# Stores of the first pass and of the output through GpSimd's queue, and G of two batches made in place by 64x32 tiles

## The chip, the core and the metric

One NeuronCore of one Trainium2 chip runs the whole program. The metric is device time in microseconds of one execution; 1384.62 us is the median of three runs of the kernel before (1382.33 to 1386.47). One further execution was recorded with a profile.

## What is computed

Attention of x and a small learned state, in both directions, then two feed-forward layers over all tokens:

```python
def attention(x, state):                      # x [8, 8, 512, 64], state [8, 8, 32, 64]
    s = x @ state.T * 0.125                   # per batch and head
    a = exp(s - s.max(-1)); a /= a.sum(-1) + 1e-9
    xread = a @ state
    s2 = state @ x.T * 0.125
    a2 = exp(s2 - s2.max(-1)); a2 /= a2.sum(-1) + 1e-9
    return concat([xread, a2 @ x], axis=2)    # 544 rows per batch

x = attention(x, state)                       # -> [4352, 512], d_model 512
h = maximum(x @ w_in, 0);   x = (h * h) @ w_out          # d_ff 2048
h = x @ w_in2;              out = (h / (1 + exp(-h))) @ w_out2
```

The four weight matrices arrive as 64-bit floats, and the kernel itself turns their words into 32-bit floats. Products are held to nearly float32 exactness: an operand is split into a rounded part "hi" and a rest "lo", and a product is three matmuls (hi by hi, lo by hi, hi by lo).

## The kernel before, in words

Work on the chip is written as calls that are only recorded. The class `Plan` keeps every operation with its engine, an estimated cost (`cost`, line 107), what it depends on, and the tiles it uses; `order` (line 220) then goes through a model of the engines and picks, one after another, the operation that can start first and is most urgent; `emit` (line 371) issues all instructions in that order. An engine runs its instructions strictly in the emitted order, so where the model is wrong about a time, an engine waits at an instruction although a later one could run. In the model, DMAs are a sixth engine, "dma", all issued by SyncE (SP): 450 ns from one issue to the next, at most 8 in flight (`LANES`), and a slack of 60 us (`DSLACK`) for a transfer that nothing urgent follows. All instructions carry line 186 in the profile, where they are recorded; they are told apart by tile names.

SBUF holds 50 pages of 128x1024 floats and 10 quads of half that size; a page is handed on only when all users of its last tile are done, and a store is a user. PSUM has eight banks: psA and psB (two each) accumulate, psC takes first products, psD takes attention.

The first pass (0 to about 660 us) makes attention and the first feed-forward layer.

- Weights. `sched_conv` (540) loads two raw pages of a weight pair (`c_load`, 490), takes absolute values on ScalarE (`c_abs`, 499), rebuilds the bits on VectorE with seven instructions (`c_bits`, 505), and adds the two parts (`c_sum`, 523) or splits them (`c_split`, 533). `c_store` (530) writes pairs of the second layer's weights to DRAM; `w1_store` (604) writes the first weight matrix for later use.
- G. Since x of the first layer is a @ state, the product with w_in is taken as a @ (state @ w_in). That inner product is called G: 256 rows (8 heads by 32 states) for each batch. `g_unit` (579) makes it for all batches out of one block of w_in: 8 matmuls of 64x64 tiles into the four banks psA and psB, four copies into "go" pages (by ScalarE or VectorE). The rows of batches 0 and 1 lie in the wrong partitions, so four DMAs in each unit move them from the go page to the page Glo of batch and quarter q (name `Glo<-go`); the rest goes to DRAM (`g<-go`) and is loaded when its batch comes (`G_load`, 610). `G_split` (622) then makes Ghi (ScalarE) and Glo (VectorE).
- `scores` (641) makes attention scores of the first three batches with 64x32 tiles, four matmuls in one bank. `sm_first` to `sm1_T` make the softmax and its transpose, the pages AThi and ATlo.
- `gemm1` (767) multiplies G by it (six matmuls into psC), `chain_a` (782) squares and splits, `gemm2` (791) multiplies by w_out in psA and psB. The first three batches (`NB`) go through d_ff in two halves (`PARTS`), so the first half needs G of q 0 and 1 only.
- `evac_a` (820) takes the sums of a Winograd scheme of seven products and stores seven blocks of a batch with 63 DMAs in all (line 838).

The second pass (660 to 1380 us) computes the second layer with those seven products: `gemm3` (968) makes and stores the hidden layer, `gemm4` (1034) makes the output; its `store` (1063) writes it out, the last block (q = 8) in two times four DMAs of 32 rows.

`arith` (451) lets the planner choose between VectorE and GpSimd for elementwise arithmetic; it is called from `split_into`, from the sums and from the softmax.

Of the kernel before, what the change touches and what calls it, by code (L numbers as in the profile page):

```python
# [10 lines left out]
F32 = mybir.dt.float32  # L11
# [16 lines left out]
class Plan:  # L28
# [3 lines left out]

    LATENCY = dict(act=dict(act=153, dve=147, pool=159, pe=265, dma=0),
                   dve=dict(act=128, dve=127, pool=155, pe=256, dma=0),
                   pool=dict(act=150, dve=150, pool=150, pe=309, dma=0),
                   pe=dict(act=197, dve=196, pool=200, pe=3, dma=0),
                   dma=dict(act=0, dve=0, pool=0, pe=100, dma=0))
    LANES = 8  # L40
    WINDOW = 25
    ROUNDS = 3

# [63 lines left out]
    def cost(self, eng, method, writes, reads, args):  # L107
        size = 1
        for ap in writes + reads:
            n = 1  # L110
            for d in ap.shape[1:]:
                n *= d
            size = max(size, n)
        psum = any(self.tiles.get(ap.tensor.name, (0, 0, ""))[2] == "ps" for ap in writes + reads)
        if eng == "dma":
            n = 1
            for d in writes[0].shape:
                n *= d
            return n * 4 / 360
        if eng == "pe":  # L120
            n = 1
            for d in writes[0].shape[1:]:
                n *= d
            if method == "transpose":
                return 109

            share = 128 * 128 // (reads[0].shape[0] * writes[0].shape[0]) if args.get("tile_position") else 1
            return max(n / 2.4 + 13, 109) * (4 if args["rhs"].dtype == F32 else 1) / share
        if eng == "act":
            return (145 if psum else 190) + size / 1.2 + (93 if "accum_out" in args else 0)  # L130
        if eng == "pool":
            return 190 + dict(tensor_tensor=2.2, memset=0.8).get(method, 3.5) * size
        fast = method in ("tensor_scalar", "tensor_copy", "memset") and not psum
        return 157 + size / (1.92 if fast else 0.96)
# [55 lines left out]
    def urgency(self, when=None):  # L190

        ops, n = self.ops, len(self.ops)
        cost = [min(f[1] for f in o["forms"]) for o in ops]
        for i, o in enumerate(ops):
            if o["forms"][0][0] == "dma":
                cost[i] += self.LEAD
        late, t = [], 0.0
        for i, o in enumerate(ops):
            if o["forms"][0][0] == "pe":
                t = when[i] + cost[i] if when else t + cost[i]  # L200
                late.append(t)
            else:
                late.append(t + (self.DSLACK if o["forms"][0][0] == "dma" else self.SLACK))
        before = [list(o["deps"]) for o in ops]
        by_tag = {}
        for t, (tag, users, space) in self.tiles.items():
            if space == "ps" and users and tag:
                by_tag.setdefault(tag, []).append(users)
        for tag, us in by_tag.items():
            us.sort(key=lambda u: u[0])  # L210
            k = self.bufs[tag]
            for a, b in zip(us, us[k:]):
                before[b[0]] += [u for u in a if u < b[0]]
        for i in reversed(range(n)):
            for d in before[i]:
                gap = self.LATENCY[ops[d]["forms"][0][0]][ops[i]["forms"][0][0]]
                late[d] = min(late[d], late[i] - cost[i] - gap)
        return [late[i] - cost[i] for i in range(n)]

    def order(self, when=None):  # L220
# [23 lines left out]
        last_end = {t: (0.0, 0.0) for t in self.tiles}  # L244
        live = set()
        now = dict(pe=600.0, act=1900.0, dve=1070.0, pool=1150.0, dma=600.0)
        ready = {e: [] for e in now}

        def add(i):
            for f in ops[i]["forms"]:  # L250
# [2 lines left out]
        for i in range(n):  # L253
            if not left[i]:
                add(i)
        lanes, hw, wire = [], 0.0, 0.0
        port = dict(dve=0.0, pool=0.0)
        head = 0
        busy, warm = deque(), False
# [3 lines left out]

        def earliest(i, eng):
            o = ops[i]
            e = now[eng]
            for d in o["deps"]:
                e = max(e, end[d] + self.LATENCY[ops[d]["forms"][form[d]][0]][eng])
            need = {}
            for t in fresh(i):  # L270
                need.setdefault(self.tiles[t][0], []).append(t)
            for tag, ts in need.items():
                ahead = 0
                for t in pending[tag]:
                    if t in ts:
                        break
                    ahead += 1
                if ahead + len(ts) > len(free[tag]):
                    return None
                e = max(e, max(x[1] for x in sorted(free[tag])[:len(ts)]) + 150)  # L280
            if eng in port and o["port"][eng]:
                e = max(e, port["pool" if eng == "dve" else "dve"])
            if eng == "dma":
                e = max(e, hw)
                if len(lanes) >= self.LANES:
                    e = max(e, lanes[-self.LANES])
            return e

        done = 0
        while done < n:  # L290
# [4 lines left out]
            for eng, cand in ready.items():  # L295
                mine = []
                low = None
                for _, i in cand[:60]:
# [8 lines left out]
                            continue  # L307
                    mine.append((e, i))
                    low = e if low is None else min(low, e)
                    if e <= now[eng] + self.PATIENCE[eng]:  # L310
                        break
                for e, i in mine:
                    if e <= low + self.PATIENCE[eng]:
                        if best is None or (e, key[i]) < best[:2]:
                            best = (e, key[i], i, eng)
                        break
# [13 lines left out]
            if eng == "pe":  # L330
# [6 lines left out]
                    busy[-1][1] = end[i]  # L337
                else:
                    busy.append([e, end[i]])
            elif eng == "dma":  # L340
                hw = e + 450
                now[eng] = e + 60
                wire = max(wire, e + 1100) + cost
                end[i] = wire + 1500
                lanes.append(end[i])
            else:
                end[i] = now[eng] = e + cost
                if eng in port and o["port"][eng]:
                    port[eng] = end[i]
            for t in o["uses"]:  # L350
                users_left[t] -= 1
                seems = e + self.DMA_SEEMS if eng == "dma" else end[i]
                last_end[t] = max(last_end[t][0], seems), max(last_end[t][1], end[i])
                if not users_left[t] and self.tiles[t][0]:
                    free[self.tiles[t][0]].append(last_end[t])
# [22 lines left out]
def attn_moe_moe_kernel(  # L378
# [12 lines left out]
    P = 128  # L391
# [19 lines left out]

    plan = Plan(dict(page=N_PAGE, quad=N_QUAD, mx1=4, mx2=4, sm1=4, sm2=4))
    V, A, G = plan.engine("dve", nc.vector), plan.engine("act", nc.scalar), plan.engine("pool", nc.gpsimd)
    T, D = plan.engine("pe", nc.tensor), plan.engine("dma", nc.sync)

    def small_tile(shape, tag):
        return plan.tile(small, shape, F32, tag, tag)
# [32 lines left out]

    def arith(op, o, a, b):
        kw = dict(out=o, in0=a, in1=b, op=op)
        plan.either((V, "tensor_tensor", kw), (G, "tensor_tensor", kw))

    def copy(o, a):
        plan.either((A, "copy", dict(out=o, in_=a)), (V, "tensor_copy", dict(out=o, in_=a)))
# [71 lines left out]
            into[key] = c  # L528

    def c_store(key, dst):  # L530
        D.dma_start(dst, cv[key].rearrange("p (k n) -> p k n", k=2))

    def c_split(key, into):
        a, c = cv.pop(key)
# [41 lines left out]

    w1p, gp = {}, {}

    def g_unit(i):
        q, p = divmod(i, 4)  # L580
        g, l = divmod(p, 2)
        pg = w1p[("w1", i // 2)][:, i % 2 * 512:(i % 2 + 1) * 512]
        for bp in range(0, 4, 2):
            ts = [acc_tile(bp), acc_tile(bp + 1)]
            for k in range(2):
                for r in range(2):
                    ps, co = slice(r * 64, (r + 1) * 64), 64 * (r ^ k)
                    T.matmul(out=ts[k][co:co + 64], lhsT=st[ps, bp + k, p].rearrange("p e n -> p (e n)"),
                             rhs=pg[ps], start=True, stop=True, tile_position=(r * 64, co))
            o2 = page(f"go{i}{bp}", F32).rearrange("p (k f) -> p k f", k=2)  # L590
            for k in range(2):
                copy(o2[:, k], ts[k])
            if bp == 0:
                for b in range(2):
                    if (b, q) not in gp:
                        gp[(b, q)] = [None, page(f"Glo{b}{q}")]
                    for r in range(2):
                        D.dma_start(f32(gp[(b, q)][1])[l * 64 + r * NS:l * 64 + (r + 1) * NS, g * 512:(g + 1) * 512],
                                    o2[r * 64 + b * NS:r * 64 + (b + 1) * NS, 0])
                D.dma_start(g_d[q][0][p], o2[:, 1])  # L600
            else:
                D.dma_start(g_d[q][1][p], o2)

    def w1_store(i):
        D.dma_start(w1_d[i], w1p.pop(("w1", i)))

    def w1_load(i):
        w1p[("s", i)] = split_page(f"w1s{i}", 1024, lambda lo: D.dma_start(lo, w1_d[i]))
# [211 lines left out]
    def evac_a(s, j, n):  # L820
# [14 lines left out]

        v.update(sums("b", v, new))
        for i in SEQ:
            at(s + 1, "dma", lambda i=i: D.dma_start(x_d[(i, j)].rearrange("(k p) n -> p k n", p=P), v[SRC_B[i]]))

    def s_tokens_split():  # L840
        hi, lo = page("srhi"), page("srlo")
# [192 lines left out]
    def gemm4(q):  # L1034
# [28 lines left out]
        def store(t, z):  # L1063
            if q < B:
                r0 = q * NT + t * 256
                D.dma_start(out[r0:r0 + 256, :].rearrange("(b p) d -> p b d", p=P), z)
            else:
                for i in range(4):
                    r0 = (4 * t + i) * NT + S
                    D.dma_start(out[r0:r0 + NS, :], z[i * NS:(i + 1) * NS, 0, :])  # L1070

        z = [new(f"z{t}") for t in range(2)]
        ls, hs = slice(0, 256), slice(256, 512)
# [70 lines left out]
    for i in range(NC // 2):  # L1144
# [9 lines left out]
        at(max(n, k + 3) + 1, "late", w1_store, i)  # L1154
        if i == 0:
            at(-12, "dma", load_st)
        at(n, "pe", g_unit, 2 * i)
        at(n, "pe", g_unit, 2 * i + 1)
    for g in range(2):
# [14 lines left out]
    for b in range(NB):  # L1174
        for q in range(4):
            n = slot(b, 4 * q)
            if b >= 2:
                at(n - 6, "dma", G_load, b, q)
            at(n - 3, "vec", G_split, b, q)

    for b in range(NB, B):
        for g in range(2):
# [115 lines left out]
```

## Time and profile before

| what | us |
|---|---|
| median of three runs | 1384.62 |
| the profiled execution | 1381.88 |
| its span, from first to last instruction | 1380.1 |
| TensorE (PE) busy | 1335.8 |
| VectorE (DVE) busy | 1056.3 |
| ScalarE (ACT) busy | 701.0 |
| GpSimd (POOL) busy | 48.9 |

The span is cut out of the profiled execution, which is 1.8 us longer. Times of instructions come from that one execution. An engine is busy from the start of an instruction to its end; "idle before" is the time that an engine stood still ahead of an instruction, with the work whose end let it go on. SPq is SyncE's queue, where all DMAs of this kernel are issued. A float32 matmul of the tiles with 64 rows is recorded as two instructions. Windows are in microseconds from the span's start.

### The profile page before, as it was taken

What the parts mean: (1) busy time and instruction counts of PE and PEld (TensorE: products, weight loads), DVE (VectorE), ACT (ScalarE), POOL (GpSimd) and SP (SyncE); (2) the same over time, 40 slices, a digit from 0 to 9 for tenths busy, and PEclk for the clock granted to TensorE, in tenths of its full rate; (3) what the DMA queues carried; (4) which work ended last, traced back from release to release, by engine and by line L of the source; (5) the groups of instructions that cost most, each with busy time, mean ns of one, the idle gap of its engine ahead of it and who ended that gap; (6) DMA issues with size and microseconds to landing.
All of it is one profiled execution on the core that took longest, in us unless ns stands there. A gap on an engine that the chain in (4) does not pass through costs nothing. (4 is left out here: it accounts for less than half of the span.)

```text
span 1380.1 us, 19261 instructions
## 1 busy us (share of the span) xinstructions
PE 1335.8 (97%) x6892; PEld 1107.9 (80%) x6892; DVE 1056.3 (77%) x1598; ACT 701.0 (51%) x1080; POOL 48.9 (4%) x41
## 2 busy tenths in 40 slices
PE   5889999999999999999999999999998999999998
PEld 1457588888888888888988888999787888888887
DVE  6979488878898888875898866777887676665664
ACT  5755776555555646554662434244455444344442
POOL 0000001110000000000020000000111000000000
PEclk9999999999999999999999999999999999999999
DMA  8761764436264546342759956667899666665663
GB/s 302 262 244 62 223 219 131 123 120 216 80 198 127 168 144 194 112 153 107 225 177 328 363 208 233 248 233 255 280 338 362 195 215 231 220 204 187 201 205 114
DMA packets 206959, 283.08 MB, mean 205 GB/s; under 512 B 13456, under 2 KB 148112, under 8 KB 206864
## 3 DMA queue, kind: packets, MB, share of 16 engines
q1 hardware_dynamic: 206864, 281.86, 61.4%
q8 instruction: 54, 0.88, 0.3%
q14 instruction: 41, 0.34, 0.1%
HBM read 161.35 MB, written 116.26 MB: 201 GB/s over the span
## 5 line engine op out<-in xcount | busy, mean ns | idle before, releaser
L186 ACT ACTIVATE rg<-psC 128x512 f32<-128x512 f32 (+1 forms) x144 | 82.6, 574 | 199.0 <-PE psC L186 195.6
L186 PE MATMUL psC<-AThi,Ghi 128*128 128x512 f32 x256 | 101.6, 400 | 6.0 <-ACT rg L186 3.1
L186 DVE TENSOR_TENSOR gact<-rg,gact 128x512 fp32r<-128x512 f32 (+1 forms) x139 | 90.9, 656 | 19.0 <-ACT rg L186 12.8
L186 PE MATMUL psC<-ATlo,Ghi 128*128 128x512 f32 x256 | 101.1, 398 | 2.2 <-DVE ATlo L186 2.2
L186 PE MATMUL psC<-AThi,Glo 128*128 128x512 f32 x256 | 101.1, 399 | 1.7 <-DVE Glo L186 1.7
L186 ACT ACTIVATE gact<-rg 128x512 fp32r<-128x512 f32 (+1 forms) x144 | 87.7, 609 | 6.9 <-DMA g<-go 3.4
L186 DVE TENSOR_TENSOR rg<-rg 128x512 f32<-128x512 f32 (+1 forms) x66 | 43.7, 662 | 48.4 <-ACT rg L186 48.0
L186 PEld LDWEIGHTS psC<-AThi,Ghi 128*128 128x128 f32 x256 | 48.1, 188 | 21.4 <-ACT AThi L186 4.6
L186 DVE TENSOR_TENSOR W<-psD,U 128x512 f32<-128x512 f32 (+2 forms) x57 | 35.4, 631 | 35.9 <-PE psD L186 35.8
L186 PEld LDWEIGHTS psC<-AThi,Glo 128*128 128x128 f32 x256 | 48.0, 188 | 16.2 <-issue 3.3
L186 PEld LDWEIGHTS psC<-ATlo,Ghi 128*128 128x128 f32 x256 | 48.2, 189 | 14.8 <-DVE ATlo L186 2.9
L186 ACT ACTIVATE r<-r 128x1024 f32<-128x1024 f32 (+2 forms) x20 | 18.6, 932 | 73.3 <-DVE r L186 61.8
L186 DVE TENSOR_SCALAR cv<-cv 128x1024 f32<-128x1024 f32 (+1 forms) x64 | 43.4, 686 | 8.2 <-ACT cv L186 7.9
L186 ACT ACTIVATE rg<-rg 128x512 f32<-128x512 f32 (+1 forms) x78 | 46.3, 594 | 0.0
L186 DVE TENSOR_TENSOR U<-psB,U 128x512 f32<-128x512 f32 (+2 forms) x57 | 35.0, 629 | 14.1 <-PE psB L186 12.6
L186 DVE TENSOR_TENSOR W<-psC,U 128x512 f32<-128x512 f32 (+2 forms) x40 | 24.2, 609 | 27.6 <-PE psC L186 27.2
L186 ACT ACTIVATE cv<-raw 128x512 f32<-128x512 f32 x64 | 40.7, 668 | 8.9 <-DMA raw<-in_w_dram 8.9
L186 PE MATMUL psA<-cc,st 64*64 64x512 f32 x128 | 25.9, 641 | 17.7 <-DVE cc L186 17.3
L186 DVE SCALAR_TENSOR_TENSOR cc<-raw,cv 128x512 int32<-128x512 int32 x64 | 41.9, 684 | 1.4 <-DMA g<-go 1.2
L186 DVE SCALAR_TENSOR_TENSOR cv<-raw,cv 128x512 f32<-128x512 uint32 x64 | 41.5, 682 | 0.2
L186 DVE TENSOR_TENSOR Glo<-Glo,Ghi 128x1024 fp32r<-128x1024 f32 x31 | 37.7, 1216 | 1.2 <-ACT Ghi L186 1.0
L186 ACT COPY U<-psA 128x512 f32<-128x512 f32 (+2 forms) x57 | 28.9, 538 | 14.9 <-PE psA L186 14.3
(1244 smaller groups left out, 4276.2 us busy)
## 6 DMA issues: line engine op xcount, KB each, us to landing
raw<-in_w_dram SPq DMA_DIRECT2D x64, 512.0 KB, 6.4
t<-s SPq DMA_DIRECT2D x36, 512.0 KB, 5.0
Glo<-g SPq DMA_DIRECT2D x96, 128.0 KB, 4.6
t<-r SPq DMA_DIRECT2D x24, 512.0 KB, 4.6
xTr<-in_xT_dram SPq DMA_DIRECT2D x16, 512.0 KB, 8.3
g<-go SPq DMA_DIRECT2D x16, 512.0 KB, 5.7
xnr<-in_xN_dram SPq DMA_DIRECT2D x16, 512.0 KB, 5.6
x<-yt SPq DMA_DIRECT2D x32, 256.0 KB, 4.0
```

Of the source, the lines that this page charges most:

```text
L186: lambda engine=engine, method=method, a=a, k=k: getattr(engine, method)(*a, **k)))
```

## The change

Stores of converted weights, of G, of the seven blocks and of the output are issued by GpSimd (`DS`) in place of SyncE (`D`). The planner gets an engine "sdma" for them: it takes GpSimd's time, 1000 ns for each (`ISSUE`), with 8 lanes of its own. `arith` is VectorE's alone, so GpSimd keeps its memsets and the DMAs. The hidden layer's stores in `gemm3` and those of `w4_sums` stay with SyncE.

For batches 0 and 1 and the quarters q 0 and 1 a new function makes G directly in the layout that `gemm1` reads: four matmuls of 64x32 tiles for each batch and block, a copy to Ghi by ScalarE and a subtraction to Glo by VectorE, both from PSUM. For these units `g_unit` leaves out the two matmuls, the copy and the four DMAs of batches 0 and 1, and `G_split` is not called for them.

```diff
+    ISSUE = 1000
...
-        ready = {e: [] for e in now}
+        clock = dict({e: e for e in now}, sdma="pool")
+        ready = {e: [] for e in clock}
...
-            elif eng == "dma":
-                hw = e + 450
-                now[eng] = e + 60
-                wire = max(wire, e + 1100) + cost
+            elif eng in self.DMA:
+                issue = 450 if eng == "dma" else self.ISSUE
+                hw[eng] = e + issue
+                now[clock[eng]] = e + (60 if eng == "dma" else issue)
+                wire = max(wire, e + 650 + issue) + cost
...
-    T, D = plan.engine("pe", nc.tensor), plan.engine("dma", nc.sync)
+    T = plan.engine("pe", nc.tensor)
+
+    D, DS = plan.engine("dma", nc.sync), plan.engine("sdma", nc.gpsimd)
...
     def arith(op, o, a, b):
         kw = dict(out=o, in0=a, in1=b, op=op)
-        plan.either((V, "tensor_tensor", kw), (G, "tensor_tensor", kw))
+        V.tensor_tensor(**kw)
...
     def c_store(key, dst):
-        D.dma_start(dst, cv[key].rearrange("p (k n) -> p k n", k=2))
+        DS.dma_start(dst, cv[key].rearrange("p (k n) -> p k n", k=2))
...
+    def direct(b, q):
+
+        return b < 2 and 4 * q < PARTS[0][1]
+
+    def g_direct(b, i):
+
+        q, g = divmod(i, 2)
+        if (b, q) not in gp:
+            gp[(b, q)] = [page(f"Ghi{b}{q}"), page(f"Glo{b}{q}")]
+        t = acc_tile(2 * b + g)
+        for l in range(2):
+            for r in range(2):
+                h, ps = 2 * l + r, slice(r * 64, (r + 1) * 64)
+                T.matmul(out=t[h * NS:(h + 1) * NS], lhsT=st[ps, b // 2, 2 * g + l, b % 2],
+                         rhs=w1p[("w1", i)][ps, l * 512:(l + 1) * 512],
+                         start=True, stop=True, tile_position=(r * 64, h * NS))
+        hi, lo = (x[:, g * 512:(g + 1) * 512] for x in gp[(b, q)])
+        A.copy(hi, t)
+        V.tensor_tensor(out=lo, in0=t, in1=hi.bitcast(F32), op=ALU.subtract)
+
     def g_unit(i):
...
         for bp in range(0, 4, 2):
+            ks = (1,) if bp == 0 and direct(0, q) else (0, 1)
             ts = [acc_tile(bp), acc_tile(bp + 1)]
-            for k in range(2):
+            for k in ks:
...
-                for b in range(2):
+                for b in range(2) if 0 in ks else ():
...
-                D.dma_start(g_d[q][0][p], o2[:, 1])
+                DS.dma_start(g_d[q][0][p], o2[:, 1])
             else:
-                D.dma_start(g_d[q][1][p], o2)
+                DS.dma_start(g_d[q][1][p], o2)
 
     def w1_store(i):
-        D.dma_start(w1_d[i], w1p.pop(("w1", i)))
+        DS.dma_start(w1_d[i], w1p.pop(("w1", i)))
...
-            at(s + 1, "dma", lambda i=i: D.dma_start(x_d[(i, j)].rearrange("(k p) n -> p k n", p=P), v[SRC_B[i]]))
+            at(s + 1, "dma", lambda i=i: DS.dma_start(x_d[(i, j)].rearrange("(k p) n -> p k n", p=P), v[SRC_B[i]]))
...
-                    D.dma_start(out[r0:r0 + NS, :], z[i * NS:(i + 1) * NS, 0, :])
+                    DS.dma_start(out[r0:r0 + NS, :], z[i * NS:(i + 1) * NS, 0, :])
...
+        for b in range(2):
+            if direct(b, q):
+                at(n, "pe", g_direct, b, i)
         at(n, "pe", g_unit, 2 * i)
         at(n, "pe", g_unit, 2 * i + 1)
...
-            at(n - 3, "vec", G_split, b, q)
+            if not direct(b, q):
+                at(n - 3, "vec", G_split, b, q)
```

## Rows read from the trace of the kernel before

**Rows 1.** The page: engine, busy us, share of the span, instructions.

```profile
PE 1335.8 (97%) x6892; PEld 1107.9 (80%) x6892; DVE 1056.3 (77%) x1598; ACT 701.0 (51%) x1080; POOL 48.9 (4%) x41
```

**Rows 2.** Windows: length; busy of PE, PEld, DVE, ACT, POOL; granted clock; DMA share; GB/s.

```profile
14.86:48.00 33.14, 28.47 (x160) 6.95 (x160) 26.18 (x44) 22.96 (x44) 0.00 (x0) 1.00 0.71 235
48.00:100.00 52.00, 42.13 (x156) 28.01 (x157) 43.72 (x66) 32.41 (x55) 1.25 (x2) 0.94 0.81 291
100.00:940.00 840.00, 837.42 (x4203) 704.83 (x4203) 675.61 (x1121) 447.54 (x743) 30.71 (x23) 1.00 0.55 182
940.00:1100.00 160.00, 154.45 (x816) 131.16 (x815) 126.06 (x157) 81.41 (x110) 14.46 (x8) 1.00 0.86 292
1340.00:1380.10 40.10, 34.42 (x198) 29.81 (x196) 19.64 (x31) 8.43 (x14) 0.00 (x0) 0.96 0.38 112
```

**Rows 3.** Waits of DVE and ACT before 105 us: total us, times, longest.

```profile
DVE go L186 <- PE psB L186: 5.7, 1, 5.7
DVE cc L186 <- ACT hi('w2', 2)_324 L186: 4.2, 1, 4.2
...
ACT Ghi L186 <- DMA w1d<-cc: 2.2, 1, 2.2
ACT hi('w2', 2)_324 L186 <- DMA g<-go: 2.0, 1, 2.0
```

**Rows 4.** SP's timeline before 105 us: start, length, what is issued.

```profile
17.49 12.71 SPq L186 DMA_DIRECT2D Glo<-go  x8
...
35.49 15.32 SPq L186 DMA_DIRECT2D Glo<-go  x22
50.85 3.94 SPq L186 DMA_DIRECT2D g<-go  x6
...
75.53 2.88 SPq L186 DMA_DIRECT2D g<-go  x3
```

**Rows 5.** PE's timeline, 25 to 81 us: start, length, instruction, count, [idle before].

```profile
25.56 1.09 PE L186 MATMUL psA<-cc,st 64*64 64x512 f32 x8
...
28.36 1.39 PE L186 MATMUL psB<-cc,st 64*64 64x512 f32 x8
...
48.01 0.73 PE L186 MATMUL psC<-AThi,Ghi 128*128 128x512 f32 x2 [1.68 <-ACT AThi L186]
...
73.14 1.04 PE L186 MATMUL psD<-xTr,st 64*32 64x512 f32 x2
74.11 0.50 PE L186 MATMUL psC<-AThi,Glo 128*128 128x512 f32 x1
74.55 1.04 PE L186 MATMUL psD<-xTr,st 64*32 64x512 f32 x2
...
79.89 1.06 PE L186 MATMUL psD<-xTr,st 64*32 64x512 f32 x8
80.89 0.72 PE L186 MATMUL psA<-gact,lo('w2', 2)_325 128*128 128x512 f32 x2
```

**Rows 6.** Groups by form: count, busy us, mean ns, idle before.

```profile
L186 DVE TENSOR_TENSOR Glo<-Glo,Ghi 128x1024 fp32r<-128x1024 f32 x31 | 37.7, 1216 | 1.2 <-ACT Ghi L186 1.0
...
L186 DVE TENSOR_TENSOR a<-psD,a 128x512 fp32r<-128x512 f32 x16 | 11.0, 690 | 4.2 <-ACT a L186 4.1
...
L186 POOL MEMSET sblk<- 128x1024 f32 x2 | 1.8, 951 | 0.0
```

**Rows 7.** Timelines of POOL, DVE and PE around 1065 us.

```profile
1064.65 2.38 POOL L186 TENSOR_TENSOR g110lo<-g110lo,g110hi 128x1024 fp32r<-128x1024 f32 x1 [23.70 <-ACT g110hi L186]
...
1064.81 2.78 DVE L186 TENSOR_TENSOR z<-R 128x512 f32<-128x512 f32 x1
...
1068.24 0.50 PE L186 MATMUL psD<-w,g040hi 128*128 128x512 f32 x1 [1.32 <-DVE W L186]
```

**Rows 8.** SP's timeline at the end of the span, last two rows.

```profile
1374.13 0.82 SPq L186 DMA_DIRECT2D out_dram<-z  x2
1375.01 2.76 SPq L186 DMA_DIRECT2D out_dram<-z  x6
```

More of the change, by code (lines that the diff above doesn't have):

```diff
@@ L28 @@
 class Plan:
[L35 to L39, printed above, removed]
+    LATENCY = dict(act=dict(act=153, dve=147, pool=159, pe=265, dma=0, sdma=153),
+                   dve=dict(act=128, dve=127, pool=155, pe=256, dma=0, sdma=128),
+                   pool=dict(act=150, dve=150, pool=150, pe=309, dma=0, sdma=150),
+                   pe=dict(act=197, dve=196, pool=200, pe=3, dma=0, sdma=197),
+                   dma=dict(act=0, dve=0, pool=0, pe=100, dma=0, sdma=0),
+                   sdma=dict(act=0, dve=0, pool=0, pe=100, dma=0, sdma=0))
+    DMA = ("dma", "sdma")
     LANES = 8
+    ISSUE = 1000
     WINDOW = 25
@@ L114, in cost @@
         psum = any(self.tiles.get(ap.tensor.name, (0, 0, ""))[2] == "ps" for ap in writes + reads)
-        if eng == "dma":
+        if eng in self.DMA:
             n = 1
@@ L194, in urgency @@
         for i, o in enumerate(ops):
-            if o["forms"][0][0] == "dma":
+            if o["forms"][0][0] in self.DMA:
                 cost[i] += self.LEAD
@@ L202, in urgency @@
             else:
-                late.append(t + (self.DSLACK if o["forms"][0][0] == "dma" else self.SLACK))
+                late.append(t + (self.DSLACK if o["forms"][0][0] in self.DMA else self.SLACK))
         before = [list(o["deps"]) for o in ops]
@@ L255, in order @@
                 add(i)
-        lanes, hw, wire = [], 0.0, 0.0
+        lanes, hw, wire = dict(dma=[], sdma=[]), dict(dma=0.0, sdma=0.0), 0.0
         port = dict(dve=0.0, pool=0.0)
@@ L265, in earliest @@
             o = ops[i]
-            e = now[eng]
+            e = now[clock[eng]]
             for d in o["deps"]:
@@ L282, in earliest @@
                 e = max(e, port["pool" if eng == "dve" else "dve"])
[L283 to L286, printed above, removed]
+            if eng in self.DMA:
+                e = max(e, hw[eng])
+                if len(lanes[eng]) >= self.LANES:
+                    e = max(e, lanes[eng][-self.LANES])
             return e
@@ L309, in order @@
                     low = e if low is None else min(low, e)
-                    if e <= now[eng] + self.PATIENCE[eng]:
+                    if e <= now[clock[eng]] + self.PATIENCE[clock[eng]]:
                         break
                 for e, i in mine:
-                    if e <= low + self.PATIENCE[eng]:
+                    if e <= low + self.PATIENCE[clock[eng]]:
                         if best is None or (e, key[i]) < best[:2]:
@@ L339, in order @@
                     busy.append([e, end[i]])
-            elif eng == "dma":
-                hw = e + 450
-                now[eng] = e + 60
-                wire = max(wire, e + 1100) + cost
+            elif eng in self.DMA:
[3 more added lines that the diff above has]
+                wire = max(wire, e + 650 + issue) + cost
                 end[i] = wire + 1500
-                lanes.append(end[i])
+                lanes[eng].append(end[i])
             else:
@@ L351, in order @@
                 users_left[t] -= 1
-                seems = e + self.DMA_SEEMS if eng == "dma" else end[i]
+                seems = e + self.DMA_SEEMS if eng in self.DMA else end[i]
                 last_end[t] = max(last_end[t][0], seems), max(last_end[t][1], end[i])
@@ L590, in g_unit @@
             o2 = page(f"go{i}{bp}", F32).rearrange("p (k f) -> p k f", k=2)
-            for k in range(2):
+            for k in ks:
                 copy(o2[:, k], ts[k])
             if bp == 0:
-                for b in range(2):
+                for b in range(2) if 0 in ks else ():
                     if (b, q) not in gp:
@@ L1065, in store @@
                 r0 = q * NT + t * 256
-                D.dma_start(out[r0:r0 + 256, :].rearrange("(b p) d -> p b d", p=P), z)
+                DS.dma_start(out[r0:r0 + 256, :].rearrange("(b p) d -> p b d", p=P), z)
             else:
```

## The prediction

> **What bounds the kernel now.** I read the engines' totals first. TensorE is busy 1335.8 of 1380.1 us, VectorE 1056.3, GpSimd 48.9 [rows 1]: the kernel can only gain where TensorE stands still, or where it runs slower than it could. So the second view is the windows, and the reader is to subtract TensorE's busy time from the length of each stretch [rows 2]. It starts at 14.86 us. From there to 48 it idles 33.14 - 28.47 = 4.7 us, from 48 to 100 it idles 9.9, from 100 to 940 only 2.6, from 940 to 1100 it idles 5.6, and 5.7 after 1340. From 48 to 100 its granted clock is also a mean of 0.94, that is, part of the stretch ran at the lower level, 1.2 GHz; that costs about 0.06 x 42.1 = 2.5 us. The head of the kernel is where this change can pay.
>
> Third, the waits of the head [rows 3]. VectorE stands still 4.2 us for the split of a weight page by ScalarE, and ScalarE waits 2.0 us there, and 2.2 elsewhere, for stores (of G, of w_in) to release a page. Fourth, SP's own timeline [rows 4] says why these stores are late: the 32 transfers Glo<-go hold the queue from 17.5 to 50.8 us, each behind its copies, and the stores of G come after them, the last issued at 78.4 us. So pages that were ready by 48 us are held for some 30 us more. VectorE idles 52.0 - 43.7 = 8.3 us between 48 and 100 [rows 2]; its conversions feed everything there.
>
> **The change, part by part.** The sum is made against the profiled execution's own 1381.88 us; the median of the runs shown is 2.7 us above it, and I add that at the end.
>
> G in place, TensorE: eight groups (two batches, four blocks) of four 64x32 matmuls are added. Standing together, such a group takes 1.0 us, from 79.89 to 80.89 [rows 5]: +8 us, or 8.5 with its recorded 1.06. Sixteen 64x64 matmuls go. Two units, 32 recorded instructions or 16 matmuls, ran from 25.56 to 29.75 us [rows 5], 0.26 us each: 4.2 us at most, and nothing if the two that are left of a step of four still take the step's time. So TensorE gets 4.3 to 8.5 us of work. It idles 4.7 us in this stretch, but partly because of order. I take the middle, 6.4 - 4.7 = 1.7, and add 0.8 because a bank is now read twice, by the copy and then by a subtraction of 0.69 us [rows 6]: the first product, now at 48.01 us [rows 5], comes **2.5 us later** (bounds 0 and +8.5).
>
> G in place, the others: VectorE loses four subtractions of 1.216 us and gets eight of 0.690 [rows 6], +0.7 us, in the term above. ScalarE's eight copies become eight roundings of the same size, and its four page-wide roundings of Ghi go. SP loses 32 issues, and nothing waits for a landing before the first product; but that product waited for AThi and not for G [rows 5], so the shorter way of G is worth nothing by itself.
>
> Stores on GpSimd, head: there are 143 of them (16 of converted weights, 32 of G, 8 of w_in, 63 of the seven blocks, 24 of the output). No row shows a DMA issued by GpSimd. Its price lies between SP's own spacing at the end, 2.76 / 6 = 0.46 us [rows 8], and GpSimd's longest instruction in the rows, 2.38 [rows 7]; I take 0.95, its memset, which like an issue reads no tensor [rows 6], and the changed planner reckons 1.0. On the whole, 143 x 0.95 = 136 us of an engine that then has nothing else. In the head the stores of q 0 and 1 (16 of G, 4 of w_in) can follow their data, and the loads behind them on SP no longer stand in line. If the pages come free in time, VectorE's 4.2 us go, and with them the pauses ahead of the slow clock, 2.5 us: **-7** (bounds 0, and -10.8 with all 8.3 us of VectorE's idle time and the clock). What is late next is VectorE itself: its busy share from 48 to 100 is 84% already. A store that waits for data on GpSimd holds only later stores, and through them pages; no loads and no arithmetic.
>
> Stores of the seven blocks, of converted weights and of all output blocks but the last: nothing. TensorE's idle time from 100 to 940 is 2.6 us, so what they hold up on SP now is covered by transfers that were issued ahead; if that cover went, 2.6 us is all there is to win.
>
> Arithmetic off GpSimd: 46.4 us of it (48.9 less 2.5 of memsets) go to VectorE at about half the time (1.216 against 2.38 for the same shape [rows 6, 7]), some 24 us over 1000. VectorE is busy 80% from 100 to 940 [rows 2], so this hides beside the matmuls; from 940 to 1100, at 79%, its 14.5 us become 7.4, and I count +0.5 (0 to +2). In return one stall goes: GpSimd's 2.38 us subtraction at 1064.65 stood beside an addition on VectorE that took 2.78 us where its size takes 0.69, and TensorE then waited 1.32 [rows 6, 7]: **-1.3** (bounds 0 and -2.1).
>
> The tail: the last eight stores start at 1374.13 on SP and are issued by 1377.77, and the span ends 2.3 us later [rows 8]. On GpSimd, 8 x 0.95 = 7.6 us from the same start is 1381.7, and with the same 2.3 the end is 1384.1, **+4.0**. Bounds: 0 at SP's price, and +6 at 1.2 us each (eight issues at 2.38 would give +15, but that row reads two full tensors and is far from an issue). Nothing covers this: no other work is left. The Trainium skill (DMA: Bandwidth & Descriptors, Specifications) gives 1 us to the first byte from GpSimd and 0.6 from SP; by its figures, an estimate, the last landing would be 0.4 us later still, +4.4. No row here shows that.
>
> Sum: +2.5 - 7 - 1.3 + 0.5 + 4.0 = -1.3: 1380.6 against 1381.88, and 1383.3 as a median of runs.
>
> **Rivals.** About 0.3% (4.2 us) is what a measurement of this kernel can tell from no change: below 1380.5 is faster, above 1388.8 slower.
>
> *The head pays in full and the tail is cheap.* VectorE's idle time goes and the issue costs what SP's does: -10.8 instead of -7 and 0 instead of +4, so -9.1, or 1375.5. For it: the waits on stores are a chain that one queue made [rows 3, 4]. Against: VectorE's longest wait, 5.7 us [rows 3], is for TensorE behind a wrong guess of the planner, and 64x32 groups are more of what was guessed wrong. Chance 0.33.
>
> *Slower: single 64x32 tiles between other matmuls.* From 73.14 us one such matmul and one of gemm1 took 1.41 us together, to 74.55 [rows 5]. The other's part is 0.20, the mean of the 4203 from 100 to 940 us [rows 2], so 1.21 against 0.25 in a group. If the planner mixes 8 of the 32 in this way, that is 8 x 0.96 = +7.7, giving 1391.0; from 6 on it decides. For it: the planner prices such a matmul at an eighth of the array and knows of no switch. Against: at that time there is little else ready to mix in. Chance 0.20.
>
> *The change doesn't do what it says: pages come free no earlier.* The planner gives stores 60 us of slack and may leave them late, or GpSimd may be held. Rows 7 show an instruction of VectorE losing 2.1 us beside one of GpSimd. If 20 issues in the head lose as much, 20 x (0.95 + 2.1) = 61 us from 17.5 ends at 78.5, where SP ends now. Then the -7 is gone: +5.7, or 1390.3. The Trainium skill (SBUF — State Buffer, Who interferes with whom) states that VectorE and GpSimd share a port pair, held for a whole instruction, and that descriptors written by GpSimd wait for it too. By that rule the loss would be as in this rival, and without it as in my sum; the trace agrees for arithmetic [rows 7], and shows nothing for a DMA. Chance 0.09.
>
> **The numbers.** The forecast gets 0.38, 0.36 of it within 0.3% and 0.02 below. Faster is 0.02 + 0.33 = 0.35, within 0.36, slower 0.20 + 0.09 = 0.29. The forecast's own range is 1379 to 1388. For 8 in 10 it must reach the rivals on both sides: down to 1372.5 (all terms at their good bounds would be 12.9 below 1384.6) and up to 1394.5 (the slower rival with the tail at its +6 and the first product 1.5 us later still).
>
> **What would show it.** Right: no wait of ScalarE for g<-go or w1d<-cc before 100 us; no wait of VectorE for the split of w2; TensorE idle from 48 to 100 down to some 4 us and granted 1.0; first product near 50 us; the last eight stores about 1 us apart on GpSimd, and a span that ends some 10 us after the first of them. Wrong: 64x32 tiles of cc standing singly among psC matmuls; GpSimd's stores of G still at 60 to 80 us; issues well under 0.9 us or over 1.2; or a first product after 55 us. A new stall from 940 to 1100, where the order is made anew as everywhere, would show that none of these terms was the one that mattered.

## The result, and the profile after

The kernel after takes 1403.97 us (median of four runs, 1399.8 to 1406.37), the kernel before 1383.47 in the runs beside it: a ratio of 1.0144, 95% interval 1.0111 to 1.0176. It is slower by 20 us. The forecast was 1383.3, and its range ended at 1394.5. The profiled run took 1404.0 us, with a span of 1402.0, so 21.9 more than the span of before. Three runs below, one each of three versions, took 2244 to 3994 us; the ratios leave them out, the medians don't.

The engines' totals of the kernel after, against [rows 1], don't show where: TensorE is busy for only 12.4 us more.

```profile
PE 1348.2 (96%) x6924; PEld 1113.8 (79%) x6924; DVE 1058.6 (76%) x1628; ACT 700.9 (50%) x1083; POOL 101.6 (7%) x151
```

The windows of the kernel after, columns as in [rows 2], with one more stretch, 1100 to 1340:

```profile
14.86:48.00 33.14, 31.24 (x152) 6.18 (x156) 20.99 (x32) 19.16 (x35) 10.58 (x15) 1.00 1.03 412
48.00:100.00 52.00, 45.56 (x197) 28.25 (x190) 47.78 (x79) 32.78 (x58) 3.06 (x5) 0.97 0.37 141
100.00:940.00 840.00, 836.43 (x4193) 704.15 (x4192) 679.10 (x1139) 451.51 (x749) 70.15 (x99) 1.00 0.54 182
940.00:1100.00 160.00, 156.27 (x836) 133.92 (x834) 127.70 (x168) 84.12 (x114) 1.44 (x2) 1.00 0.88 298
1100.00:1340.00 240.00, 225.66 (x1264) 195.63 (x1263) 146.07 (x160) 90.61 (x98) 8.58 (x12) 0.98 0.61 195
```

The same stretch of the kernel before, which the prediction never asked for:

```profile
1100.00:1340.00 240.00, 238.91 (x1367) 207.13 (x1367) 157.56 (x172) 102.37 (x111) 0.00 (x0) 1.00 0.65 212
```

Subtract busy time from length in each. From 48 to 100 TensorE idles 6.4 us in place of 9.9, from 940 to 1100 3.7 in place of 5.6: small gains. From 1100 to 1340, where the output is made, it idles 14.3 us in place of 1.1, runs 103 fewer matmuls in the same time, and part of the stretch is granted the lower clock. A second way to see it is to follow one tile through both traces: when TensorE first multiplies it (us).

| first matmul on | before | after | later by |
|---|---|---|---|
| Ghi (first product) | 48.0 | 57.3 | 9.3 |
| x01hi (second pass) | 706.2 | 706.6 | 0.4 |
| g010hi (output stage) | 1033.9 | 1036.5 | 2.6 |
| g410hi | 1195.0 | 1203.6 | 8.6 |
| g710hi | 1313.8 | 1330.3 | 16.5 |
| g810hi (last block) | 1352.5 | 1374.0 | 21.5 |
| end of the span | 1380.1 | 1402.0 | 21.9 |

The head loses nine microseconds and has them back when the first pass ends. Nearly all of the loss is taken in the output stage, one to five microseconds in each block from the third on (g210hi is still on time, at 1116.2 before and 1116.1 after). From there to the end of the span, before and after:

```profile
1116.20:1380.10 263.90, 257.13 (x1470) 222.83 (x1468) 166.75 (x190) 105.52 (x119) 0.00 (x0) 0.99 0.62 199
```

```profile
1116.10:1402.00 285.90, 262.59 (x1464) 227.21 (x1463) 163.51 (x188) 102.56 (x118) 13.24 (x21) 0.97 0.57 181
```

Of the 22.0 us more, 16.5 are idle time (23.3 in place of 6.8), and 5.5 are longer busy time for nearly the same number of matmuls, at a mean granted clock (third number from the end) of 0.97 in place of 0.99.

What does TensorE wait for there? Its largest wait after 1100 us (total us, times, longest) in the kernel after, second here, and the same wait in the kernel before, first:

```profile
PE psA L186 <- ACT U L186: 1.1, 2, 0.8
```

```profile
PE psA L189 <- ACT U L189: 16.9, 6, 4.2
```

U is a plain copy of a sum by ScalarE. The chain of waits of the kernel after, for 1240 to 1266 us, leads from it back to the store:

```profile
1244.75 6.38 DMA out_dram<-z
...
1251.14 0.36 SPq L189
...
1253.04 7.82 DMA g530lo<-t
...
1260.96 1.04 ACT g530hi L189
1262.00 0.49 ACT U L189
...
1262.54 0.50 PE psA L189
```

The load of g551lo needs the page that the first output store of this stretch (z of q = 4) holds. The loads of g540lo, g541lo and g530lo stand behind it on SP, ScalarE's rounding of g530 waits for the last of them, and the copy U stands behind that on ScalarE. Now compare the head of this chain. SP's timeline in the kernel before:

```profile
1234.41 0.38 SPq L186 DMA_DIRECT2D out_dram<-z  x1
1234.84 0.47 SPq L186 DMA_DIRECT2D g550lo<-t  x1
1238.19 0.36 SPq L186 DMA_DIRECT2D g551lo<-t  x1
```

In the kernel after, GpSimd's timeline (the store) and SP's (the loads):

```profile
1244.75 0.72 POOL L189 DMA_DIRECT2D out_dram<-z  x1 [34.14 <-DVE z L189]
```

```profile
1244.37 0.36 SPq L189 DMA_DIRECT2D g550lo<-t  x1
1251.14 0.36 SPq L189 DMA_DIRECT2D g551lo<-t  x1
```

The same two stores in the DMA views, with the time from issue to landing last (us), before and after:

```profile
out_dram<-z SPq DMA_DIRECT2D x1, 512.0 KB, 3.9
```

```profile
out_dram<-z POOLq DMA_DIRECT2D x1, 512.0 KB, 6.4
```

Over the first stores of six blocks (those next to the loads of g250lo to g750lo) it is a mean of 4.2 us before and 6.1 after. Before, the load of g550lo stood 0.43 us behind the store in the same queue; now it goes 0.38 us ahead of it on another.

The load of g551lo follows the store's issue by 6.39 us after, and by 3.78 before; but in the kernel before it does not wait for the store. From SP's waits at 1238.1 us:

```profile
SPq L186 <- PE psC L186: 3.1, 1, 3.1
```

There the page goes to the next load, g540lo, 4.53 us behind the store. Some expectations below take the 3.8 us for the page's return on SP; the landing, 4.2, is the right number.

### The profile page after: what moved, and what is told of

Same layout as the page of the kernel before. It is cut to its first block, busy times and chain, and to the rows that moved or that the text cites. A ratio compares the mean times of both kernels' runs of the same rounds, so it can differ in the third digit from the quotient of the medians.

```text
span 1402.0 us, 19330 instructions
## 1 busy us (share of the span) xinstructions
PE 1348.2 (96%) x6924; PEld 1113.8 (79%) x6924; DVE 1058.6 (76%) x1628; ACT 700.9 (50%) x1083; POOL 101.6 (7%) x151
## 4 chain that ended last, share of the span: by engine, by line
PE 50%; issue 39%; DMA 3%; DVE 1%; POOL 1%; ACT 1%; SPq 0%; POOLq 0%; ACTq 0%; DVEq 0%
PE psC L189 16%; PE psA L189 15%; PE psB L189 13%; PE psD L189 5%; DMA g630lo<-t 1%; POOL out_dram L189 1%; DMA g730lo<-t 1%; DMA g530lo<-t 1%; DMA g750lo<-t 0%; DMA out_dram<-z 0%; POOL x L189 0%; DVE sm L189 0%; ACT rg L189 0%; SPq L189 0%; ACT U L189 0%
## 5 line engine op out<-in xcount | busy, mean ns | idle before, releaser
L189 DVE TENSOR_TENSOR gact<-rg,gact 128x512 fp32r<-128x512 f32 (+1 forms) x144 | 94.6, 658 | 19.6 <-ACT rg L189 15.9
L189 DVE TENSOR_TENSOR rg<-rg 128x512 f32<-128x512 f32 (+1 forms) x59 | 38.6, 655 | 48.1 <-ACT rg L189 47.7
L189 POOL DMA_DIRECT2D out_dram<-z x24 | 15.4, 644 | 666.5 <-DVE z L189 666.5
L189 PEld LDWEIGHTS psC<-AThi,Ghi 128*128 128x128 f32 x256 | 47.9, 188 | 16.9 <-ACT AThi L189 4.1
L189 PE MATMUL psB<-cc,st 64*64 64x512 f32 (+1 forms) x160 | 35.5, 628 | 16.4 <-DVE cc L189 14.8
L189 ACT ACTIVATE rg<-rg 128x512 f32<-128x512 f32 (+1 forms) x85 | 50.9, 598 | 0.1
```

Source lines behind the costliest of these rows:

```text
L189: lambda engine=engine, method=method, a=a, k=k: getattr(engine, method)(*a, **k)))
```

## The experiments

Which part costs the 20 us? First the output stores alone, taken back from the change, and then put alone into the kernel before.

**Output stores back on SP** (all else as after; the planner knows it):

```diff
-    DS.dma_start(out[r0:r0 + 256, :].rearrange("(b p) d -> p b d", p=P), z)
+    D.dma_start(out[r0:r0 + 256, :].rearrange("(b p) d -> p b d", p=P), z)
```

The last block's stores likewise.

> The changed kernel, with only the output's stores back on SyncE. Theory 1 (page chain): in the last stage the loads of g wait for the page of the block's last z, and a store on GpSimd gives it back about 3 us later than one on SyncE (6.8 against 3.8 us from z to the load behind it); seven blocks make the loss. Then this kernel ends within 1382 to 1388 us, TensorE's waits for ACT U after 1100 us fall from 16.9 to under 3 us, and what is left of a loss is the 2.6 us by which the last stage starts late. Theory 2 (order): the planner's new order of the last stage is at fault whatever queue it uses; since the planner orders this one anew too, 1382 to 1404. Theory 3 (the loss comes from the first pass, G in place or the arithmetic): still 1400 to 1406.

Measured: 1381.26 us, ratio to before 0.9984 (0.9975 to 0.9993). Without these 24 stores the rest of the change is worth -0.16%, a little better than the 1382 to 1388 that was expected. TensorE's waits for ACT U after 1100 us fall to 3.2 us, just over the expected 3.

**The kernel before, its order untouched, with only the output stores issued by GpSimd:**

```diff
+    DO = plan.engine("dma", nc.gpsimd)
...
-                D.dma_start(out[r0:r0 + 256, :].rearrange("(b p) d -> p b d", p=P), z)
+                DO.dma_start(out[r0:r0 + 256, :].rearrange("(b p) d -> p b d", p=P), z)
```

> The kernel before, order untouched on every engine; only the output's stores are issued by GpSimd instead of SyncE, which the planner isn't told. Theory 1 (page chain): about 3 us for each of seven blocks, 1398 to 1406 us, and waits of TensorE for ACT U of 14 to 20 us after 1100. Theory 2 (order): no change, 1381 to 1386, but for the tail. Theory 3: 1381 to 1386.

Measured: 1403.67 us, ratio 1.0146 (1.0129 to 1.0163): the whole loss, with only the queue of 24 stores changed. TensorE's waits after 1100 us have the row of the kernel after:

```profile
PE psA L186 <- ACT U L186: 16.6, 6, 3.7
```

**The order of after, output stores physically on SP:**

```diff
+    DO = plan.engine("sdma", nc.sync)
```

> The changed kernel's order on every engine, with the output's stores issued by SyncE in that same order. Theory 1 (page chain): the pages come back 3 us sooner, so 1383 to 1389 us. Theory 2 (order): 1399 to 1406, as with the stores on GpSimd. Theory 3: 1399 to 1406.

Measured, a single run: 1380.04 us, below the 1383 to 1389 that was expected. The new order is not at fault; the queue is. Nor is it the load that gets the page: here and in the first run above g551lo waits for the store on SP, as it does for the one on GpSimd, and nothing is lost.

Why does the queue matter: through the page that the store holds, or through GpSimd's time to issue it?

**Output in half tiles that hold no page** (after, stores on GpSimd; z in four quads in place of two pages, each half stored when it is ready):

```diff
-        arith(ALU.add, z, a[:, :, 0:256], a[:, :, 256:512])
+        zz = quad(f"z{t}{h}")[:, :c * 256].rearrange("p (b n) -> p b n", b=c)
+        arith(ALU.add, zz, a[:, :, 0:256], a[:, :, 256:512])
```

> The changed kernel with the output's stores still on GpSimd, but z in four half-size tiles of the other pool, which nothing else uses in the last stage, each stored by itself; no load waits for a store of the output any more. Theory 1 (page chain): 1380 to 1387 us, no wait of SP for out_dram, waits of TensorE for ACT U after 1100 us under 3 us. Theory 2 (order): anything from 1382 to 1404, not tied to these waits. Theory 3: 1400 to 1406. If GpSimd's issue itself slows other engines: over 1390.

Measured: 1382.39 us, ratio 0.9992 (0.998 to 1.0004). GpSimd now issues twice as many stores in these blocks, and the loss is gone. The window of the output stage:

```profile
1100.00:1340.00 240.00, 236.68 (x1354) 205.33 (x1353) 153.32 (x169) 99.39 (x108) 16.84 (x24) 1.00 0.64 206
```

TensorE's idle time is 3.3 us in place of 14.3, and no load waits for an output store. So the store costs through its page and not by its issue. Why then does the page come free so late? Either a store by GpSimd is slow, or any store that leaves SP's queue is.

**The kernel before, output stores issued by ScalarE:**

```diff
+    DO = plan.engine("dma", nc.scalar)
```

> The kernel before, order untouched; only the output's stores are issued by ScalarE, whose queue is a hardware one like SyncE's but another one. On GpSimd, with this order, the load behind a block's last z but one was issued 6.1 us after the store (mean of six blocks), on SyncE 3.8. Theory S (GpSimd's queue is slower by itself): 3.8 to 4.5 us here and 1382 to 1389 us. Theory C (any second queue: the load of the next g is no longer held behind the store, goes ahead of it and shares the transfer engines with it): 5.5 to 6.5 us and 1395 to 1404 us. Half of each: about 5 us and 1389 to 1395. ScalarE waiting at the store for z may add a few us under either.

Measured: 1401.06 us, ratio 1.0120 (1.0105 to 1.0135). Its SP and ScalarE timelines at the same place:

```profile
1243.74 0.36 SPq L186 DMA_DIRECT2D g550lo<-t  x1
...
1249.66 0.36 SPq L186 DMA_DIRECT2D g551lo<-t  x1
```

```profile
1243.75 0.46 ACTq L186 DMA_DIRECT2D out_dram<-z  x1
```

From the store to the load that takes its page it is 5.91 us, and a mean of 5.9 over six blocks, against 6.1 with the stores on GpSimd in the order of before; on SP such a store lands after 4.2. ScalarE as the second queue loses 16.4 us to the kernel before that was run beside it, GpSimd 20.2, so about a fifth of the harm at most is GpSimd's own. The remaining idea is the place in the line: on SP the store stood ahead of g(q)50lo and went first. Two runs try it from both sides.

**All on SP, but in each block the load issued first, then the store:**

```diff
+                if t == 1:
+                    plan.marked.append(len(plan.ops))
...
+            seq[a:b + 1] = seq[a + 1:b + 1] + [s]
```

Here s is the first store of a block, a its place in the emitted order `seq`, and b that of the next DMA.

> The kernel before with all DMAs on SP, and only these two issues exchanged in each block: the load first, then the store. Theory (place in the queue): the loss appears without any second queue; the store ends 2 to 3 us later, the page comes free some 6 to 7 us after the issue, and the time is 1395 to 1405. Rival (only the queue that issues the store counts): 1381 to 1387, as before.

Measured: 1386.07 us, ratio 1.0016 (1.0003 to 1.0028). By its time this is the rival's. Yet the stores land late, as the theory has it. Here is its SP timeline, then ScalarE's, then the landing of the store in the first:

```profile
1236.21 0.36 SPq L186 DMA_DIRECT2D g550lo<-t  x1
1236.62 0.50 SPq L186 DMA_DIRECT2D out_dram<-z  x1
1239.97 0.36 SPq L186 DMA_DIRECT2D g551lo<-t  x1
```

```profile
1243.07 1.05 ACT L186 CAST g550hi<-g550lo 128x1024 fp32r<-128x1024 f32 x1 [3.35 <-DMA out_dram<-z]
```

```profile
out_dram<-z SPq DMA_DIRECT2D x1, 512.0 KB, 6.4
```

With no second queue, a store 0.41 us behind a load lands 6.4 us after its issue, and a mean of 6.3 over the six blocks, in place of 4.2 before. But the exchange also changed who gets the page: no load waits for it here, ScalarE's rounding to g550hi does, 6.4 us after the issue. It waits 3.35 us for that, and the run is only 1.6 us slower than the kernel before. My expectation of 1395 to 1405 left that out. That a late page is dear where a load takes it, because the loads behind stand in the same line, is read from these traces; no run with all DMAs on SP gave such a late page to a load.

**Output stores on GpSimd, and the load that followed the first of them on GpSimd too, behind it** (order of before):

```diff
+            own[l] = dict(engine=self.second)
```

Here l is the DMA that followed the store, and `second` is GpSimd.

> The kernel before with its output stores issued by GpSimd, and the load that follows the first store of each block (g150lo ... g750lo and the like) issued by GpSimd too, right behind the store in the same queue. Theory (what was lost is the store's place ahead of that load in one queue): the store has the transfer engines to itself again, the next load gets its page some 4.2 to 4.8 us after the store's issue in place of 6.1, and the time falls back to 1384 to 1392. Rival (a store in any other queue than SP's is slow by itself): the page still takes 6 us, and the time stays at 1400 to 1407.

Measured: 1395.86 us, ratio 1.0087 (1.007 to 1.0103): neither range. Its GpSimd and SP timelines, and the landings of the store shown and of this block's second one, at 1252.20:

```profile
1246.28 0.72 POOL L186 DMA_DIRECT2D out_dram<-z  x1 [35.47 <-DVE z L186]
1247.09 0.77 POOL L186 DMA_DIRECT2D g550lo<-t  x1
```

```profile
1249.54 0.36 SPq L186 DMA_DIRECT2D g551lo<-t  x1
```

```profile
out_dram<-z POOLq DMA_DIRECT2D x1, 512.0 KB, 3.2
```

```profile
out_dram<-z POOLq DMA_DIRECT2D x1, 512.0 KB, 8.9
```

The step from the first store to the load of g(q)51lo falls to a mean of 3.9 us over six blocks (3.3 to 4.9), and the store lands as quickly as on SP, 3.9 against 4.2. A first store by GpSimd is as quick as one by SP when the load of g(q)50lo stands behind it. The second store of a block is not: it lands in a mean of 8.0 us, against 6.5 with the stores alone on GpSimd and 5.5 before. And only part of the loss comes back: the time fell from 1403.67 to 1395.86, still 11.4 us above the kernel before.

**The load behind the second store on GpSimd too:**

```diff
-                if t == 1:
-                    plan.marked.append(len(plan.ops))
+                plan.marked.append(len(plan.ops))
```

> As the run before last (the kernel before, output stores and the load behind the first store on GpSimd), and the load that follows the second store of each block (g230lo ... g730lo) on GpSimd as well, behind that store. Theory (each store that shares the transfer engines with loads of another queue lands late): the second store too lands in some 4 to 5 us in place of up to 8.9, and the time falls from 1395.9 to 1385 to 1391, what is left being GpSimd's later issue (0.4 us for the store, 0.8 for the load behind it, in each of seven blocks). Rival (what remained there is GpSimd's issue and nothing else): 1394 to 1400, no better for the second load.

Measured: 1398.15 us, ratio 1.0118 (1.0093 to 1.0143), inside the rival's range and no better than the run above. The second stores land in a mean of 6.9 us, not in the 4 to 5 that the theory wanted. From g010hi to g810hi the profiled run takes 332.3 us, against 333.6 with one load behind, 340.6 with the stores alone on GpSimd and 318.6 before; the times of single runs differ by more than these two do (1393.92 to 1400.66 in the run above). So the place in the line explains the first store's landing and some 9 of the 20 us. What is left of the loss in these two runs is not settled: the second store still lands late, GpSimd issues the store some 0.4 us after VectorE's last addition, SP within 0.05, and the moved loads another 0.8 later, but no run has taken one of these away alone.

Now the rest of the change.

**After, output stores on SP, without G in place** (all units by `g_unit`):

```diff
-        return b < 2 and 4 * q < PARTS[0][1]
+        return False
```

> The changed kernel with the output's stores on SyncE and without G in place (batches 0 and 1 by DMA again). Theory H1 (as predicted: G in place puts off the first product of 128 rows, and the early stores win it back): first product at 46 to 50 us, last stage no later than in e1, 1375 to 1380 us. Theory H2 (taking the 32 transfers Glo<-go off SyncE's queue is what wins it back, and the store queue alone wins nothing): 1381 to 1385.

Measured: 1376.37 us, ratio 0.9939 (0.9922 to 0.9955): faster than both kernels. Its first product:

```profile
47.66 0.73 PE L189 MATMUL psC<-AThi,Ghi 128*128 128x512 f32 x2 [1.66 <-ACT AThi L189]
```

It reaches x01hi at 701.9 us; the kernel before does at 706.2.

**The kernel before with G in place and nothing else:**

```diff
+        for b in range(2):
+            if direct(b, q):
+                at(n, "pe", g_direct, b, i)
         at(n, "pe", g_unit, 2 * i)
```

> The kernel before with G in place alone; all stores on SyncE and the arithmetic free to go to GpSimd. H1: first product at 55 to 59 us, the second pass starts at 709 to 716 instead of 706, 1386 to 1394 us. H2: first product at 55 to 59 us, but the second pass starts by 707, 1380 to 1384 us.

Measured: 1383.75 us, ratio 0.9993 (0.998 to 1.0007). Its first product comes at 56.79 us, 8.8 later than before, and x01hi at 706.0, no later. Alone, G in place costs nothing at the end; beside the early stores it costs some 5 to 6 us: the version with it is 2.2 us below the kernel before that was run beside it, the one without it 8.3, and the medians differ by 1381.26 - 1376.37 = 4.9. Why the first pass makes up the delay in one case and not in the other, I haven't separated.

**Output stores on SP and half tiles:**

```diff
-    DS.dma_start(out[r0:r0 + 256, hs].rearrange("(b p) d -> p b d", p=P), zz)
+    D.dma_start(out[r0:r0 + 256, hs].rearrange("(b p) d -> p b d", p=P), zz)
```

> e1 (output's stores on SyncE) with z in four half-size tiles of the other pool. If waits on the output's pages still cost something on SyncE's queue (TensorE idles 3.2 us for ACT U after 1100 us in e1): 1376 to 1380 us. If that queue with twice the stores holds up the loads instead: 1382 to 1386. If neither: 1380 to 1382, like e1.

Measured: 1382.02 us, ratio 0.9988 (0.9976 to 0.9999), no better than the page tiles on SP at 0.9984. On SP the store's page was free in time.

## Why the prediction was wrong

**The step that failed** is "Stores of the seven blocks, of converted weights and of all output blocks but the last: nothing." Its reason was TensorE's small idle time from 100 to 940 us, "covered by transfers that were issued ahead". For the output blocks, which lie after 1074 us, that is a row of another stage; and a stage that idles little may do so because a chain in it just fits. Here the chain had hardly any slack: a store issued behind a finished block, a page that comes free some 4 us later, the loads from there on, a rounding, a copy. With 6 us at its head it no longer fits, and TensorE pays 16.9 us in six waits, most of the rest in matmuls at the lower clock (0.97 in the mean from g210hi on, 0.99 before). The prediction asked of each moved store what stands behind it on its queue, and answered with the issue: loads "no longer stand in line". It did not ask what the store loses when a load no longer stands behind it. "A store that waits for data on GpSimd holds only later stores, and through them pages; no loads and no arithmetic" is the same slip: a page that is held too long holds the load that needs it. The words "if that cover went, 2.6 us is all there is to win" priced only a gain.

**Stores in the head.** -7 was forecast (0 to -10.8). With them (and the arithmetic on VectorE), but without G in place and with the output on SP, the second pass begins 4.3 us earlier, and the kernel is 0.6% faster: right in sign and near in size, for that version; no run takes the stores and the arithmetic apart. No wait of ScalarE for g<-go or w1d<-cc is left before 105 us in the kernel after, as the prediction said, so the rival by which pages come free no earlier is excluded.

**G in place.** +2.5 us at the first product (0 to +8.5) was forecast, and it is +9.3, beyond the bound. The windows up to the first product, before and after:

```profile
14.86:48.01 33.15, 28.47 (x160) 6.95 (x161) 26.19 (x44) 22.97 (x44) 0.00 (x0) 1.00 0.71 235
```

```profile
14.82:57.26 42.44, 38.44 (x193) 7.85 (x193) 27.63 (x47) 25.73 (x48) 12.74 (x19) 1.00 1.03 413
```

TensorE is busy for 10.0 us more and idles 0.7 us less (4.0 in place of 4.7). The sum took 6.4 us of work and let the whole 4.7 us of idle time take it up; both were off. One reason for the first is a bound that the prediction named itself, "nothing if the two that are left of a step of four still take the step's time": four matmuls into psA take 1.09 us in [rows 5], and in the kernel after two take as long:

```profile
24.09 1.07 PE L189 MATMUL psA<-cc,st 64*64 64x512 f32 x4
```

The prediction also missed a wait on VectorE. From the waits before 105 us of the kernel after, and from VectorE's timeline:

```profile
DVE Glo L189 <- ACT Ghi L189: 13.9, 3, 9.2
```

```profile
31.69 0.69 DVE L189 TENSOR_TENSOR Glo<-psA,Ghi 128x512 fp32r<-128x512 f32 x1 [9.17 <-ACT Ghi L189]
```

The rounding that it waits for, and the four matmuls (eight records) ahead of that, from ScalarE's timeline and TensorE's:

```profile
31.09 0.57 ACT L189 CAST Ghi<-psA 128x512 fp32r<-128x512 f32 x1
```

```profile
29.91 1.06 PE L189 MATMUL psA<-cc,st 64*32 64x512 f32 x8
```

VectorE's order puts this subtraction ahead of the next conversions of the weights, and TensorE reaches its matmuls only at 29.91 us. So VectorE stands still from 22.5 to 31.7 with those conversions queued behind. The kernel before with G in place alone has the same row:

```profile
31.01 0.69 DVE L186 TENSOR_TENSOR Glo<-psA,Ghi 128x512 fp32r<-128x512 f32 x1 [8.54 <-ACT Ghi L186]
```

So the prediction counted the second reader of the bank (0.8 us), and not whom it waits for. Whether this wait adds to the first product's delay is open: TensorE does not idle more for it, and no run removed it alone.

**The tail.** +4.0 was forecast (0 to +6). GpSimd's timeline at the end:

```profile
1395.20 3.95 POOL L189 DMA_DIRECT2D out_dram<-z  x8 [14.64 <-DVE z L189]
```

The span ends 6.8 us after the first of the last eight stores, before 6.0: +0.8. An issue of 32 rows took 3.95 / 8 = 0.49 us, about SP's 0.46 and half of the 0.95 that I took.

**The stall at 1065 us and the arithmetic.** -1.3 and +0.5 were forecast. TensorE idles 1.8 us less from 940 to 1100. Together these terms were right in sign, and decided nothing; no run separates them.

**The slower rival**, single 64x32 tiles, had the sign and not the place: by x01hi the head had lost 0.4 us. The sentence under "Wrong" came nearest: a new stall where the order is made anew. But it named 940 to 1100, and the run with the order of before shows that the order had no part in it. Two other signs under "Wrong" came true, a first product after 55 us (57.3) and issues under 0.9 us (0.49 to 0.72); neither bears on the loss.

## What to carry to other kernels

Before a store is moved to another queue, look for who takes its buffer: if it is a load, the store's landing time is on that load's path, and its place ahead of other loads in the old queue is worth something that no engine's busy time shows (here 4.2 us to its landing in place of 6.1). A stage with almost no idle time is to be read on its own before "nothing" is written, by the chain of waits through its buffers and not by the idle time of its neighbours. Where such a move is wanted for the issuing queue's sake, give the stored tile a buffer that no load waits for, or leave those stores where they are: here the fastest version has 119 stores on GpSimd and these 24 on SP.

## What the runs showed of the hardware that I had not expected

The first output store of a block (512 KB, mean of six blocks) lands in 4.2 us on SP and in 3.9 on GpSimd when the load of g(q)50lo stands behind it in the same queue; in 6.3 us on SP when that load is ahead, and in 6.1 on GpSimd when that load goes ahead of it on SP. For these stores the order among queued transfers was worth 2.1 to 2.2 us, the choice of queue 0.2 to 0.3. The second stores don't show it so plainly: 5.5 us before, 6.5 on GpSimd, 8.0 and 6.9 in the two runs with moved loads. The Trainium skill (DMA: Bandwidth & Descriptors, Issuing engines are not separate DMA queues) says that DMAs started by several engines run on the same 16 DMA engines and interleave, and that starting them on more engines saves only the time to initiate them. The trace agrees that they share (6.1 us to the landing in place of 4.2, beside a load on another queue), and shows what a store on a second queue can cost: 20 us here.

GpSimd's issue took 0.72 us for a full output store and 0.49 for one of 32 rows. SP's issues of the full stores took 0.38 to 0.47, its issues of 32 rows 0.46; GpSimd's shortest instruction in [rows 6, 7], a memset, takes 0.95.
